# An attention block followed by an MLP on one core: modulation rows in a list of their own, other start conditions for weight preparation, and later reload times

## The chip, the cores and the metric

The kernel runs on one core of a Trainium2 chip. The core has a matrix engine (PE, with its weight loads shown as PEld), a vector engine (DVE), a scalar engine (ACT), a general engine (POOL) and an engine that issues the transfers (SP). The metric is the device time of one execution in microseconds. Three timed runs of the kernel before are given, and one further execution was profiled.

## The reference

One sequence of 2048 tokens of width 512. Six rows of modulation come from `c`; then attention with 32 heads of 16, and a mixer with a shift along the sequence and an MLP of width 1792.

```python
mod = (silu(c) @ w_mod).reshape(1, 6, 1, 512)
sa, ca, ga, sb, cb, gb = mod[:, 0], ..., mod[:, 5]
h = layernorm(x) * (1 + ca) + sa
x = x + ga * attention(h, wqkv, wo)          # 32 heads, softmax over 2048 keys
h = layernorm(x) * (1 + cb) + sb
y = h + shifted(gelu(layernorm(h) @ w1)) @ w2    # four groups of channels, shifts +1, -1, +2, -2
y = y + gelu(layernorm(y) @ w3) @ w4
return x + gb * y
```

## The kernel before

Everything is float32 in, float32 out. To multiply float32 matrices, each operand is split into a high part and a low rest, and three products are summed (`mm3`, L322 to L327). So each weight must be prepared once: loaded, split by ACT (high part) and DVE or POOL (rest). The attention weights stay in SBUF for their stage (`wp`, two buffers). The MLP weights and wo are cut into 20 `pieces` of two halves each, split, stored to a scratch tensor `Ws`, and read back later through a ring (`wr`).

**Stages.** A prologue normalizes x and prepares K of the first four heads. Then 64 attention units follow, in the order of four chunks of 512 queries by 16 pairs of heads. A unit has 16 steps: for each, two score matmuls (L956), two exponentials on ACT (L952), two products for the row maxima of a later unit (L940) with DVE reductions (L936), a halving of the low parts on POOL (L1004, or on ACT, L121) and the products with v (L1029, L1026). Beside the first 16 units ("the first quarter") lie the rest of the Q, K and V projections, the modulation rows and the weight pieces. Beside the other 48 units lies the MLP of the chunk just finished (`tail`), and after unit 63 the last chunk's MLP stands alone.

**Order.** No engine order comes from the compiler. The program itself holds a planner, `Sched` (L78 on): for each engine it keeps a planned time `T`, and instructions are emitted in the planned order. The attention steps are fixed; everything else is written as generators (lists of work that yield their PE cost or a condition) and as chains of operations for ACT, DVE and POOL. `fill` gives the generators a PE allowance after each block; `one` runs the first generator in the list whose condition holds, so earlier generators go first. `after(t, fn)` runs `fn` once the planned PE time reaches t. `dma` gives an estimated landing time: its size at 360 bytes per ns, behind SP's earlier transfers, plus 2200 ns (`DBW, DLAT`). All transfers are issued by SP, in the order in which they are emitted; a transfer whose buffer is still being read holds up what is behind it.

`drain(flag)` lets the planner step on, without attention work, until a flag is set. At the end of the first quarter it does that for v 1, kq 3, q 0, q 1 and `pieces` (L1529 on).

**Names.**
- `todo`: the projections in order: v 0, kq 1, kq 2, v 1, kq 3, q 0, q 1 (L790). `weights_gen` prepares their weights, `qkv_gen` computes them. There are two lists of the latter: (0, 3) and (1, 2, 4, 5, 6). v 0 and v 1 are the two halves of v; kq g is K of eight heads and Q of the first chunk for them.
- `staged` (L406): takes one of five buffers `wst`, issues a load into it and returns the planned landing time. All weight preparation and the modulation rows use it.
- `mod_gen` (L596): modulation rows, four pieces of 128 columns each, four matmuls per piece, result by DVE to `garow`, `sbrow`, `cbrow` or `gbrow`. `garow` and `sbrow` are the same tile: the first is used up by wo's pieces before the second is written.
- `pieces_load` (L802): loads the halves in the order w1, w3, wo, w2, w4. Before wo it makes `garow`, before w4 the other three rows. `pieces_gen` (L819): takes one of three buffers `wq`, then the scale by `vcol` (wo only, ACT, L831), by the row (wo and w4, POOL, L833), the high part (ACT, L843), the rest (POOL, L844), two stores.
- `load_v` (L912): reloads one quarter of v (`vst`) for the next unit, called through `sch.after` in `pv_part` (L1037).

Of the kernel before, what the change touches and what calls it, by code (L numbers as in the profile page):

```python
# [55 lines left out]
LATE = 1e9  # L56
# [7 lines left out]
NPT = 8  # L64
PLOAD = 3500.0
WLAT = 4000.0
WSR = 1
DBW, DLAT = 360.0, 2200.0
NST = 5
NWQ = 3  # L70
# [211 lines left out]
def cA(n=CH):  # L282
    return n / 1.2 + 52
# [11 lines left out]
def kernel(ctx, tc, A_x, A_wqkv, A_wo, B_w1, B_w2, B_w3, B_w4, c, w_mod, out):  # L295
# [58 lines left out]
    vcol = con.tile([P, 4], F32, name="vcol")  # L354
# [3 lines left out]
    cbrow = con.tile([P, D], F32, name="cbrow")  # L358
    sbrow = con.tile([P, D], F32, name="sbrow")
    gbrow = con.tile([P, D], F32, name="gbrow")  # L360
# [19 lines left out]
    sch = Sched()  # L380
    done = set()
# [18 lines left out]
    garow = sbrow  # L400
# [5 lines left out]
    def staged(src3):  # L406

        yield lambda: wst
        t = wst.pop(0)
        f = t.bitcast(F32)  # L410
        o = 0
        n = sum(x.shape[2] for x in src3)
        f3 = f.rearrange("p (k n) -> p k n", n=n)
        for x in src3:
            e = sch.dma(dma.dma_start, f3[:, :, o:o + x.shape[2]], x)
            o += x.shape[2]
        return t, f3, e

    def split_chain(t, hi, lo, *ops):
        f = t.bitcast(F32)  # L420
# [362 lines left out]

    def weights_gen():
        for i, (_, wt, a) in enumerate(todo):
            yield lambda: i <= ready["done"] + (("kq", 0) in done)
            ready[i] = yield from wt(a)


# [3 lines left out]
    def qkv_gen(*ids):  # L793
        for i in ids:
            gen, _, a = todo[i]
            yield lambda: i in ready
            yield from gen(ready.pop(i), a)
            ready["done"] += 1

    loaded = []  # L800

    def pieces_load():  # L802
        yield lambda: ("v", 0, 2) in done
        for i, (nm, src, nk, n) in enumerate(pieces):
            if i == order["wo"][0]:
                yield lambda: ("vcol", 0) in done and ("vcol", 1) in done
                yield from mod_gen((2, garow, 0.0))
            if i == order["w4"][0]:
                yield lambda: len(wqs) == NWQ and not loaded
                yield from mod_gen((3, sbrow, 0.0), (4, cbrow, 1.0), (5, gbrow, 0.0))  # L810
            src3 = kpn(src)
            for c in range(2):
                yield sch.wait(PLOAD)
                yield lambda: len(wst) > WSR or len(ready) + ready["done"] > len(todo)
                t, _, e = yield from staged([src3[:, c:c + 1] if nk == 2 else src3[:, 2 * c:2 * c + 2]])
                loaded.append((i, nm, c, t, e + WLAT))
        loaded.append(None)

    def pieces_gen():  # L819
        while True:  # L820
            yield lambda: loaded and wqs
            x = loaded.pop(0)
            if x is None:
                break
            i, nm, c, t, e = x
            w = wqs.pop(0)
            f = t.bitcast(F32)
            ops = []
            if nm == "wo":
                k = 2 * (i - order["wo"][0]) + c  # L830
                ops.append(("A", cA(), lambda f=f, k=k: act.activation(f, f, AF.Copy, scale=vcol[:, k:k + 1])))  # L831
            if nm in rows:
                ops.append(("G", cG(), lambda f=f, r=rows[nm]: pool.tensor_tensor(f, f, r, op=OP.mult)))  # L833

            def gone(t=t, w=w):
                wst.append(t)
                wqs.append(w)

            def store(i=i, c=c, w=w, f=f, gone=gone):
                for h, t in enumerate((w.bitcast(F32), f)):  # L840
                    e = sch.dma(dma.dma_start, Ws[i][:, h, 512 * c:512 * c + 512], t)
                sch.after(e, gone)
            sch.chain(*ops, ("A", cA(), lambda f=f, w=w: act.activation(w, f, AF.Copy)),  # L843
                      ("G", cG(), lambda f=f, t=t, w=w: pool.tensor_tensor(t, f, w, op=OP.subtract)),  # L844
                      (None, 0, store), ready=e)
        yield lambda: len(wqs) == NWQ
        done.add("pieces")

    def drain(flag):
# [17 lines left out]
    for ci in range(NC):  # L867
# [2 lines left out]
        ("A", cA(), lambda i=i: act.activation(hi[:, 2 * i:2 * i + 2], w0f[:, 2 * i:2 * i + 2], AF.Copy)),  # L870
        ("D", cD(), lambda i=i: dve.tensor_tensor(lo[:, 2 * i:2 * i + 2], w0f[:, 2 * i:2 * i + 2], hi[:, 2 * i:2 * i + 2],
                                                  op=OP.subtract)))], mark("w0"), ready=arr["w0"])
    for g in (mod_cols(), bounds(), ln1_T(), qk_first(hi, lo), weights_gen(), qkv_gen(0, 3), qkv_gen(1, 2, 4, 5, 6)):
        sch.add(g)
    drain(("q", 0, 0))
    for ci in range(NC):
# [26 lines left out]
    def load_unit(u):  # L903
# [3 lines left out]
        for j in range(2):  # L907
            h = 2 * pr + j
            load_rows(q, j, Qs, h, cs, slice(0, CH))
            load_rows(kst[u % 3], j, Ks, h, slice(0, S), slice(0, S))  # L910

    def load_v(u, i):  # L912

        if u < NU:
            sch.dma(dma.dma_start, vst[i], Vs[units[u][1], :, 4 * i:4 * i + 4])

    sm = Slots(NSM)
# [93 lines left out]
    def pv_part(s, lo):  # L1011


        u, kt = divmod(s, NKT)
        if kt == 0 and not lo:
            pv[u] = ap_.tile([P, CH], F32, name="pv", tag="v", bufs=1)
        v, acc = vst[kt // 4], pv[u]

        def mms():
            for j in range(2):  # L1020
                for i in range(2):
                    r = 64 * j + 32 * i
                    if lo:
                        n = 9 + DH if i else 1 + DH
                        c = 128 + 32 * j + 9 + DH
                        te.matmul(acc[r:r + n, :], v[:, (kt + i) % 4, c - n:c].bitcast(F16), pt[s + i].bitcast(F16)[:, j, 0::2],  # L1026
                                  start=False, stop=kt == NKT - 2, skip_group_check=True)
                    else:
                        te.matmul(acc[r:r + 32, :], v[:, kt % 4, r:r + 32], pt[s].bitcast(F16)[:, j, 1::2],  # L1029
                                  start=kt == 0, stop=False, skip_group_check=True)  # L1030
        e = sch.put("P", CCOL, 0.0, mms)
        if lo:
            for i in range(2):
                pts.append(pt.pop(s + i))
                e_low.pop(s + i)
            if kt % 4 == 2:
                sch.after(e + 300, partial(load_v, u + 1, kt // 4))  # L1037
            if kt == NKT - 2:
                acs.append((u, e + COUT))

# [391 lines left out]

    sch.share(sm, MOST0)
    sch.add(pieces_load(), 0)
    sch.add(pieces_gen(), 0)

    def budget(s):
# [36 lines left out]
    for k, blk in enumerate(blocks + [[]] * (LAG + CPER)):  # L1474
        if LENDS in blk:
            sch.most = MOST
        for x in blk:
            if x % 2 == 0:
                before(x // 2)
                if x >= 0 and x % 32 == 0:  # L1480
                    drain(("shift", x // 32))
        if acs:
            ac_copy()
        row = [divmod(x, 2) for x in blk if x < 2 * NS]
        s0 = row[0][0] if row else 0
        col = []
        if k >= LAG and (k % CPER == 0 or not blk):

            x = (blocks[min(k - LAG, len(blocks) - 1)] or [-1])[-1]
            while pvs and 2 * (pvs[0][0] + pvs[0][1]) < x:  # L1490
                if col and blk and pvs[0][0] % NKT == 0 and not pvs[0][1]:
                    break
                col.append(pvs.pop(0))
        t, start = CIN, 0.0
        need = sum((s >= 0) + (s + LEAD < NS) for s, _ in row)
        sch.flush(need)
        banks = sorted(sm.t)
        n = 0
        for s, i in row:
            n += (s >= 0) + (s + LEAD < NS)  # L1500

            start = max(start, banks[n - 1 + 2 * (s < 0)] - t)
            t += CROW
        t += CMID
        for s, i in col:
            start = max(start, pv_ready(s, i) - t)
            t += CCOL
        sch.gap(start)
        sch.flush(need)
        sch.T["P"] = max(sch.T["P"], start) + CIN  # L1510
        low = sorted(e_exp)
        for s, i in row:
            for fn in row_pair(s, i):
                fn()
        for s in low:
            p_low(s)
        sch.T["P"] += CMID
        for s, i in col:
            pv_part(s, i)
        if col:  # L1520
            sch.T["P"] += COUT
        for e in "ADG":
            sch.misc(e, max(sch.T["P"], sch.T[e]) + TOLE[e])
        due += sum(budget(x // 2) / 2 for x in blk) if blk else 3 * TAILB[-1] / 2
        if k % CPER == CPER - 1 or s0 < 0:
            sch.fill(due)
            due = 0.0
        if blk and blk[-1] == 2 * (NS // NC) - 1:
            for key in (("v", 1), ("kq", 3), ("q", 0), ("q", 1), "pieces"):  # L1529
                drain(key)  # L1530
            qpx.close()
            tpx = ExitStack()
            tp[0] = tpx.enter_context(tc.tile_pool(name="tp", bufs=1, side="right"))
# [47 lines left out]
```

## Time and profile before

| what | value |
|---|---|
| median of three runs | 2119.67 us (2115.31 to 2126.15) |
| profiled execution | 2129.35 us, span of its instructions 2127.6 us |
| granted TensorE clock, mean | 0.958 |

```profile
PE 1963.1 (92%) x14464; PEld 1163.4 (55%) x14464; DVE 1648.0 (77%) x2936; ACT 1536.5 (72%) x3320; POOL 1716.3 (81%) x1657
```

The line is the share of the span in which each engine was busy, with its number of instructions. It is a mean over stages that differ: the prologue to about 100 us, the first quarter to about 610 us, three more quarters to about 1960 us, and the last MLP. In the lines of the profile, L12 is line 12 of the program; a matmul carries the line of the helper that issues it (L323, L325, L327 are the three products of `mm3`), so groups are told apart by the tiles they write and read. A line such as "ACT pt L952 <- PE mb L940" says that the first waited for the second.

### The profile page before, as it was taken

What the parts mean: (1) busy time and instruction counts of PE and PEld (TensorE: products, weight loads), DVE (VectorE), ACT (ScalarE), POOL (GpSimd) and SP (SyncE); (2) the same over time, 40 slices, a digit from 0 to 9 for tenths busy, and PEclk for the clock granted to TensorE, in tenths of its full rate; (3) what the DMA queues carried; (4) which work ended last, traced back from release to release, by engine and by line L of the source; (5) the groups of instructions that cost most, each with busy time, mean ns of one, the idle gap of its engine ahead of it and who ended that gap; (6) DMA issues with size and microseconds to landing.
All of it is one profiled execution on the core that took longest, in us unless ns stands there. A gap on an engine that the chain in (4) does not pass through costs nothing.

```text
span 2127.6 us, 41619 instructions
## 1 busy us (share of the span) xinstructions
PE 1963.1 (92%) x14464; PEld 1163.4 (55%) x14464; DVE 1648.0 (77%) x2936; ACT 1536.5 (72%) x3320; POOL 1716.3 (81%) x1657
## 2 busy tenths in 40 slices
PE   6979897999859999999999999999989999999899
PEld 4645564554325555555545455555545555555788
DVE  7768686888749887888999888888898878882654
ACT  6367677767846877877868887877768797887353
POOL 4368788878887998988978999989879898998442
PEclk9989998999869998999999999999999999999999
DMA  5786876655573354454633444544534444443432
GB/s 194 187 248 203 222 185 195 177 144 144 144 252 93 88 127 100 136 118 136 155 66 87 108 100 108 138 117 108 172 96 104 108 104 108 112 121 101 176 138 85
DMA packets 228514, 292.69 MB, mean 138 GB/s; under 512 B 121264, under 2 KB 172976, under 8 KB 212016
## 3 DMA queue, kind: packets, MB, share of 16 engines
q1 hardware_dynamic: 228304, 290.02, 50.3%
q8 instruction: 115, 1.88, 0.4%
q14 instruction: 95, 0.78, 0.1%
HBM read 226.49 MB, written 62.91 MB: 136 GB/s over the span
## 4 chain that ended last, share of the span: by engine, by line
PE 58%; ACT 13%; DVE 13%; DMA 5%; POOL 5%; issue 3%; SPq 2%; POOLq 0%; ACTq 0%; DVEq 0%
PE mb L940 12%; PE pv L1029 9%; PE sc L956 9%; DVE mx L936 8%; ACT pt L952 7%; PE w L323 6%; PE w L325 5%; PE w L327 5%; PE pv L1026 4%; POOL pt L1004 2%; SPq L100 2%; DMA kst<-Ks 1%; DMA wst<-in_A_wqkv_dram 1%; PE ot L1056 1%; ACT pt L121 1%
## 5 line engine op out<-in xcount | busy, mean ns | idle before, releaser
L1004 POOL TENSOR_SCALAR pt<-pt 128x1024 f16<-128x1024 uint16 x983 | 1307.4, 1362 | 167.7 <-ACT pt L952 162.9
L936 DVE TENSOR_REDUCE mx<-mb 128x1 f32<-128x512 f32 x2048 | 1280.2, 683 | 209.6 <-PE mb L940 160.7
L952 ACT ACTIVATE pt<-sc 128x512 int32<-128x512 f32 x2048 | 1080.4, 607 | 303.7 <-PE mb L940 243.9
L940 PE MATMUL mb<-kst,qtl 48*128 48x512 f32 x2048 | 766.5, 462 | 90.2 <-ACT pt L952 49.1
L956 PE MATMUL sc<-qtl,kst 64*128 64x512 f32 x2048 | 733.5, 452 | 21.5 <-DMA qtl<-nm 8.8
L940 PEld LDWEIGHTS mb<-kst,qtl 48*128 48x128 f32 x2048 | 354.9, 197 | 302.8 <-ACT pt L952 113.8
L956 PEld LDWEIGHTS sc<-qtl,kst 64*128 64x128 f32 x2048 | 344.1, 190 | 183.3 <-ACT pt L952 55.1
L1029 PE MATMUL pv<-pt,vst 128*32 128x512 f16 x4096 | 366.4, 405 | 0.4 <-DMA vst<-Vs 0.4
L1026 PE MATMUL pv<-pt,vst 128*17 128x512 f16 (+1 forms) x2048 | 215.2, 403 | 0.3 <-ACT pt L121 0.2
L1029 PEld LDWEIGHTS <-vst 128*32 128x32 bf16 x4096 | 92.0, 96 | 164.1 <-issue 107.6
L323 PE MATMUL w<-A,wr 128*128 128x256 f32 (+2 forms) x576 | 176.4, 306 | 1.6 <-ACT A L317 1.4
L325 PE MATMUL w<-A,wr 128*128 128x256 f32 (+2 forms) x576 | 174.2, 302 | 1.1 <-DVE A L313 0.8
L1315 POOL TENSOR_TENSOR g<-xs,g 128x256 fp32r<-128x256 f32 (+2 forms) x144 | 103.4, 721 | 86.0 <-ACT g L1314 85.6
L327 PE MATMUL w<-A,wr 128*128 128x256 f32 (+2 forms) x576 | 172.3, 299 | 0.0
L323 PEld LDWEIGHTS w<-A,wr 128*128 128x128 f32 x576 | 113.4, 197 | 23.9 <-issue 13.9
L325 PEld LDWEIGHTS w<-A,wr 128*128 128x128 f32 x576 | 113.4, 197 | 19.3 <-issue 16.8
L327 PEld LDWEIGHTS w<-A,wr 128*128 128x128 f32 x576 | 113.5, 197 | 12.1 <-issue 12.1
L323 PE MATMUL w<-wr,g 128*128 128x512 f32 x288 | 119.5, 415 | 0.0
L327 PE MATMUL w<-wr,g 128*128 128x512 f32 x288 | 117.8, 409 | 0.3 <-POOL g L1315 0.3
L325 PE MATMUL w<-wr,g 128*128 128x512 f32 x288 | 116.6, 405 | 0.0
L1324 DVE SCALAR_TENSOR_TENSOR sq<-sq,w 128x256 f32<-128x256 f32 (+1 forms) x108 | 43.5, 403 | 80.2 <-ACT xs L1320 73.1
L1330 POOL TENSOR_TENSOR xs<-xs,sq 128x256 f32<-128x256 f32 (+1 forms) x108 | 75.8, 703 | 14.6 <-ACT sq L1329 14.0
(145 smaller groups left out, 2192.2 us busy)
## 6 DMA issues: line engine op xcount, KB each, us to landing
wr<-Ws SPq DMA_DIRECT2D x80, 1024.0 KB, 5.9
vst<-Vs SPq DMA_DIRECT2D x256, 192.0 KB, 2.7
kst<-Ks SPq DMA_DIRECT2D x126, 384.0 KB, 6.7
qtl<-Qs SPq DMA_DIRECT2D x128, 96.0 KB, 5.0
Vs<-vt SPq DMA_DIRECT2D x32, 384.0 KB, 4.8
Ws<-wq SPq DMA_DIRECT2D x40, 256.0 KB, 4.3
Ws<-wst SPq DMA_DIRECT2D x40, 256.0 KB, 4.2
wst<-in_B_w_dram SPq DMA_DIRECT2D x36, 256.0 KB, 4.2
```

Source lines behind the costliest of these rows:

```text
L323: te.matmul(o, lh, rh, start=first, stop=False)
L325: te.matmul(o, lh, rl, start=False, stop=False)
L327: te.matmul(o, ll, rh, start=False, stop=last)
L936: end = sch.crit("D", 605, e + PX, lambda: dve.reduce_max(mxs[u][:, j, g, c:c + 1], b, axis=AX.X))
L940: return ready, lambda: te.matmul(b, lhs, kst[u % 3][r, c * CH:(c + 1) * CH], start=True, stop=True), after
L952: ea = sch.crit("A", 480, e + PX, lambda: act.activation(pt[s][:, j], b, AF.Exp))
L956: return ready, lambda: te.matmul(b, kst[u % 3][r, kt * P:(kt + 1) * P], qst[u][r], start=True, stop=True), after
L1004: e_low[s] = XP["G"] + sch.crit("G", 1345, ready, lambda: pool.tensor_scalar(o, i, 0.5, 1.0, op0=OP.mult, op1=OP.mult))
L1026: te.matmul(acc[r:r + n, :], v[:, (kt + i) % 4, c - n:c].bitcast(F16), pt[s + i].bitcast(F16)[:, j, 0::2], start=False, stop=kt == NKT - 2 ...
L1029: te.matmul(acc[r:r + 32, :], v[:, kt % 4, r:r + 32], pt[s].bitcast(F16)[:, j, 1::2], start=kt == 0, stop=False, skip_group_check=True)
L1315: ("G", cG(n), lambda: pool.tensor_tensor(lo, xs, hi, op=OP.subtract)), (None, 0, end))
L1330: ("G", cG(n), lambda: pool.tensor_tensor(xs, xs, sq, op=OP.mult)), *tail_ops, bank=b)
```

## The change

Five parts, in the words of the diff:

1. The modulation rows get a generator of their own, `mod_rows`, which starts when kq 1 is done and goes ahead of the pieces in the list. It makes ga, gb and cb, then waits until wo's halves are stored, and makes sb. `pieces_load` waits for ga before wo and for gb before w4, and its start moves from three quarters of v 0 to kq 2.
2. The order of the projections: one list (1, 2, 3, 4, 5, 6) after v 0, so v 1 comes after kq 2 instead of in a list beside it; a weight is prepared when the projection two places ahead of it is done.
3. `staged` returns a landing time that is 4000 ns later (`WLAT`). For the pieces that is as before, where the same amount was added by `pieces_load`; for the projections and the modulation rows it is new.
4. v's reload is put 5000 ns (`VLATE`) behind the planned end of its readers, instead of 300 ns; should its first reader come sooner, it is issued there.
5. In the wait for a bank before the first score, a bank that has no planned end is left out of account.

```diff
+VLATE = 5000.0
...
-        return t, f3, e
+        return t, f3, e + WLAT
...
-            yield lambda: i <= ready["done"] + (("kq", 0) in done)
+            yield lambda: i < 1 or (("kq", 0) in done if i == 1 else ("todo", i - 2) in done)
             ready[i] = yield from wt(a)
...
             ready["done"] += 1
+            done.add(("todo", i))
...
+    def mod_rows():
+        yield lambda: ("kq", 1) in done
+        yield from mod_gen((2, garow, 0.0))
+        done.add("garow")
+        yield from mod_gen((5, gbrow, 0.0))
+        done.add("gbrow")
+        yield from mod_gen((4, cbrow, 1.0))
+        yield lambda: all(("wo", 2 * i + c) in done for i in order["wo"] for c in range(2))
+        yield from mod_gen((3, sbrow, 0.0))
+        done.add("mods")
+
     def pieces_load():
-        yield lambda: ("v", 0, 2) in done
+        yield lambda: ("kq", 2) in done
         for i, (nm, src, nk, n) in enumerate(pieces):
             if i == order["wo"][0]:
-                yield lambda: ("vcol", 0) in done and ("vcol", 1) in done
-                yield from mod_gen((2, garow, 0.0))
+                yield lambda: ("vcol", 0) in done and ("vcol", 1) in done and "garow" in done
             if i == order["w4"][0]:
-                yield lambda: len(wqs) == NWQ and not loaded
-                yield from mod_gen((3, sbrow, 0.0), (4, cbrow, 1.0), (5, gbrow, 0.0))
+                yield lambda: "gbrow" in done
...
-                loaded.append((i, nm, c, t, e + WLAT))
+                loaded.append((i, nm, c, t, e))
...
                 sch.after(e, gone)
+                done.add((nm, 2 * i + c))
...
-        yield lambda: len(wqs) == NWQ
+        yield lambda: len(wqs) == NWQ and "mods" in done
         done.add("pieces")
...
-    for g in (mod_cols(), bounds(), ln1_T(), qk_first(hi, lo), weights_gen(), qkv_gen(0, 3), qkv_gen(1, 2, 4, 5, 6)):
+    for g in (mod_cols(), bounds(), ln1_T(), qk_first(hi, lo), weights_gen(), qkv_gen(0), qkv_gen(1, 2, 3, 4, 5, 6)):
...
+    vnext = set()
+
     def load_v(u, i):
-        if u < NU:
+        if (u, i) in vnext or not u:
+            vnext.discard((u, i))
             sch.dma(dma.dma_start, vst[i], Vs[units[u][1], :, 4 * i:4 * i + 4])
...
+        load_v(u, kt // 4) if (u, kt // 4) in vnext else None
         v, acc = vst[kt // 4], pv[u]
...
-                sch.after(e + 300, partial(load_v, u + 1, kt // 4))
+                if u + 1 < NU:
+                    vnext.add((u + 1, kt // 4))
+                sch.after(e + VLATE, partial(load_v, u + 1, kt // 4))
...
     sch.add(pieces_load(), 0)
+    sch.add(mod_rows(), 0)
     sch.add(pieces_gen(), 0)
...
-            start = max(start, banks[n - 1 + 2 * (s < 0)] - t)
+            free = banks[n - 1 + 2 * (s < 0)]
+            start = max(start, (free if free < LATE else banks[n - 1]) - t)
```

More of the change, by code (lines that the diff above doesn't have):

```diff
@@ L837, in gone, with store @@
                 wqs.append(w)
-            def store(i=i, c=c, w=w, f=f, gone=gone):
+            def store(i=i, c=c, w=w, f=f, gone=gone, nm=nm):
                 for h, t in enumerate((w.bitcast(F32), f)):
```

## The prediction, made before the changed kernel was timed

> **What bounds the kernel now.** I first read the share of busy time by engine and the waits, then stretches of the span one by one, because the first quarter (attention units 0 to 15, beside which the weights are prepared) differs from the other three.
>
> ```profile
> 187.80:349.10 161.30, 141.19 (x1112) 84.89 (x1110) 115.45 (x203) 120.64 (x259) 134.55 (x120) 0.96 0.78 213
> 382.70:561.90 179.20, 169.71 (x1340) 90.41 (x1338) 149.91 (x264) 129.86 (x260) 151.06 (x127) 0.98 0.56 144
> 205.00:584.00 379.00, 346.26 (x2664) 191.83 (x2668) 295.98 (x515) 279.48 (x571) 317.00 (x272) 0.96 0.66 174
> 584.00:609.40 25.40, 0.79 (x9) 0.00 (x0) 0.17 (x1) 6.16 (x11) 20.96 (x18) 0.50 0.76 272
> 609.40:640.00 30.60, 28.69 (x202) 15.25 (x202) 24.27 (x42) 21.91 (x44) 25.25 (x22) 0.86 0.83 240
> 640.00:1090.00 450.00, 430.78 (x3333) 242.95 (x3326) 379.00 (x672) 351.89 (x784) 395.90 (x390) 0.96 0.46 116
> 1560.00:1960.00 400.00, 384.38 (x2983) 216.34 (x2984) 306.23 (x547) 320.58 (x704) 360.08 (x350) 0.98 0.42 105
> ```
>
> Columns: stretch, its length, busy time of PE, PEld, DVE, ACT, POOL, granted TensorE clock, DMA share, GB/s. In the later quarters PE is busy for 384.4 of 400 us: there the kernel is bound by PE, with POOL (90%) and ACT (80%) close behind. In the first quarter it is not: from 205 to 584 us PE is busy only 91%, and from 584 to 609 us it stands still. PE's timeline, with the gap before an instruction in brackets, names the holes:
>
> ```profile
> 137.08 1.28 PE L940 MATMUL mb<-kst,qtl 48*128 48x512 f32 x2 [8.27 <-ACT pt L952]
> ...
> 259.48 0.79 PE L604 MATMUL mr<-wst,sil 128*128 128x128 f32 x3 [4.07 <-DMA wst<-in_w_mod_dram]
> ...
> 349.75 1.12 PE L1056 MATMUL ot<-ident,ac 128*128 128x128 f32 x4 [11.16 <-ACT ac L1045]
> ...
> 609.44 0.79 PE L940 MATMUL mb<-kst,qtl 48*128 48x512 f32 x1 [24.65 <-ACT pt L952]
> ```
> These four gaps make 48.2 us. "ACT pt" is only the last link. Behind the first and the 11.2 us one ACT itself sat on a weight that had not landed:
>
> ```profile
> 135.91 0.63 ACT L425 ACTIVATE wp<-wst 128x512 fp32r<-128x512 f32 x1 [6.16 <-DMA wst<-in_A_wqkv_dram]
> ...
> 341.82 0.63 ACT L843 ACTIVATE wq<-wst 128x512 fp32r<-128x512 f32 x1 [1.76 <-DMA Ws<-wq]
> 346.58 0.63 ACT L425 ACTIVATE wp<-wst 128x512 fp32r<-128x512 f32 x1 [4.12 <-DMA wst<-in_A_wqkv_dram]
> 348.58 0.63 ACT L425 ACTIVATE wp<-wst 128x512 fp32r<-128x512 f32 x1 [1.38 <-DMA wst<-in_A_wqkv_dram]
> ```
>
> Behind the 24.65 us gap the chain that ended last shows something else: the quarter's end drains `pieces`, and the MLP weight halves are scaled (L833) and split (L844) on POOL one after the other, with attention halted.
>
> ```profile
> 583.59 1.94 POOL wst L833 x2
> 585.52 0.45 issue
> 585.97 1.28 POOL wst L844
> ...
> 588.47 1.41 POOL wst L844 x2
> ...
> 607.02 1.23 POOL wst L833
> 608.27 0.63 ACT wq L843
> 608.90 0.49 ACT pt L952
> ```
>
> Why they are late is seen when the work on `wq` (one ACT operation for each of the 40 halves) and on `mr` (matmuls of the modulation rows, eight for each of 16 row pieces) is counted by stretch:
>
> ```profile
> 100.00:205.00 105.00, 6.84 (x11) 13.40 (x11) 0.93 0.77 222
> 205.00:390.00 185.00, 9.70 (x15) 21.27 (x16) 0.94 0.77 210
> 390.00:530.00 140.00, 0.00 (x0) 0.00 (x0) 1.00 0.55 140
> 530.00:584.00 54.00, 3.26 (x5) 6.38 (x5) 0.90 0.55 137
> 584.00:612.00 28.00, 5.66 (x9) 11.37 (x9) 0.50 0.75 266
> ```
> ```profile
> 390.00:530.00 140.00, 13.54 (x96) 11.85 (x96) 3.38 (x12) 1.00 0.55 140
> ```
>
> For 140 us no half is touched (x0), since the list of pieces stands in its own generator behind 12 modulation row pieces (96 matmuls). Of the last 14 halves five are split by 584 us, and nine fall into the drain.
>
> **The change, part by part.** *Rows by their own list, and pieces later.* `pieces_load` starts when kq 2 is done instead of after three quarters of v 0, so about 198 us instead of 115:
>
> ```profile
> 115.52 0.42 SPq L100 DMA_DIRECT2D wst<-in_B_w_dram  x1
> ...
> 194.88 0.90 SPq L100 DMA_DIRECT2D Qs<-qk  x2
> ```
> ```profile
> 123.24 0.62 ACT L843 ACTIVATE wq<-wst 128x512 fp32r<-128x512 f32 x1
> ```
>
> The first load of a half is the 115 us one; the stores at 194.9 us are kq 2's last, and land some 3 us later. The 140 us pause goes. None of the new conditions is a wait on an engine; they only hold back the planner's lists, so nothing queues behind them. So 40 halves have 198 to 584 us = 386 us, 9.6 us each. Before, 26 halves went through by 390 us; the 11 of the first row took about 82 us from the first at 123 us, 7.5 us each; 40 x 7.5 = 300 us, and at 8.6 (15% worse, since the weights of v 1, kq 3 and q share the five `wst` buffers) 344 us, ending at 542 us. I expect the drain to be empty. With the halves move their 120 transfers on SP's queue (a load and two stores each), past the loads of K, Q and v; DMA share is 0.55 to 0.77 there, so I give that no price of its own. The twelve row pieces (13.5 us PE, 3.4 us DVE in the 140 us) move from 390 to 530 to about 130 to 350 us with the same instructions: 0.
>
> The work itself stays and now lies beside attention. From 205 to 609.4 us, 404.4 us, PE is busy 346.3 + 0.8 = 347.1 us, POOL 317.0 + 21.0 and ACT 279.5 + 6.2, together 623.7. To it come the 11 halves that were done before 205 us: 13.4 POOL + 6.8 ACT, making 643.9. Two floors follow. By PE: 347.1 at the share of the last stretch (384.38 / 400 = 0.961) is 361 us. By POOL and ACT together, between which the planner moves the low halves of pt: 643.9 at (360.08 + 320.58) / 400 = 1.70 is 378 us; at the 1.66 of 640 to 1090 us it is 388 us. The higher floor decides; I take 378, so **-26 us**, ends 361 (-43) and 395 (-9; the rate of the worst of these rows with one hole left). This contains the drain and the holes at 259 and 349 us.
>
> *v half 1 after kq 2, not beside it.* It is due in unit 7, about 355 us, and its 16 tiles start after kq 2, at 198 us, against 191 before. The instructions are the same, so 0; what hides the delay is that slack of over 150 us. If it were used up, attention would stand in a drain for v as it does for the pieces (nearest row: 24.65 us).
>
> *Arrival 4 us later for all weights.* Of ACT's 6.16 us wait at 136 us at most 4 go, so the PE gap of 8.27 shrinks by 4: **-4 us** (ends 0 and -8). The modulation rows get it too (the PE gap of 4.07 us at 259 us), but that lies in the term above. In the prologue the same 4 us delays kq 1 and v 0, while q and k of group 0 occupy PE: **+1 us** (0 to 4).
>
> A rule speaks against this term. First the trace, issues with their size and the median time to landing:
>
> ```profile
> wst<-in_B_w_dram SPq DMA_DIRECT2D x36, 256.0 KB, 4.2
> ...
> wst<-in_w_mod_dram SPq DMA_DIRECT2D x16, 256.0 KB, 5.2
> ...
> wst<-in_A_wqkv_dram SPq DMA_DIRECT2D x8, 256.0 KB, 7.2
> ```
>
> The planner counts 0.7 + 2.2 us for them. The Trainium skill, page "DMA: Bandwidth & Descriptors", section "Anatomy of one DMA — SWDGE (gpsimd) path", fits a copy at 2.0 us plus its bytes at 436 GB/s, an estimate of 2.6 us for 256 KB; by it the old figure is ample, the term would be 0 and the sum 2089 us. The medians above, 4.2 to 7.2 us, disagree.
>
> *Clock behind the holes.* From 609.4 to 640 us the granted clock is 0.86; 14% of 30.6 us is 4.3 us; I take **-3 us** (0 to -5). The Trainium skill, "TensorE: Matmul & The Clock Gate", Part 1, says that an idle window of some 3.4 us halves the clock until a busy window of that length has passed; by it each of the four holes costs some 1.7 us after its end, an estimate of 7 us in all, and a sum of 2081 us. The 0.50 in the row of 584 us agrees with the halving.
>
> *v's reload 5 us later.* What SP waits for, and what PE waits for through SP:
>
> ```profile
> SPq L100 <- PE pv L1026: 704.7, 167, 11.1
> SPq L100 <- PE w L327: 186.1, 45, 22.7
> ```
> ```profile
> PE sc L956 <- DMA qtl<-nm: 8.8, 7, 1.8
> ```
> ```profile
> vst<-Vs SPq DMA_DIRECT2D x256, 192.0 KB, 2.7
> ```
>
> SP's queue stands for 705 us behind v's readers, but what PE loses to queued transfers is small: 8.8 us at the shift rows. Behind a v load stand shift rows, K and Q of the next unit and `wr`. Half of 8.8, less what the first term holds: **-3 us** (0 to -6). SP will in part only wait for the next item (the L327 row). The fallback for a bank that is taken concerns rows before the first score alone: 0.
>
> **Sum:** -26 - 4 + 1 - 3 - 3 = -35 us. The profiled execution took 2129.35 us (span 2127.6, 1.8 around it), 9.7 above the median of the three timed runs, 2119.67; the terms are differences, so I subtract them from the median: **2085 us**.
>
> **Rivals.** (1) *POOL and ACT take it back.* The halves come back as delays of exponentials and low halves. For it: POOL is the second engine everywhere, and 187.8 to 349.1 us, where pieces, v and kq 3 ran together, shows 84% on POOL with PE at 88%. Against: (134.55 + 120.64) / 161.3 = 1.58 leaves room up to 1.70. At 395 us for the stretch and nothing else but -4 and -3: 2119.7 - 16 = 2104 us.
> (2) *The issue is late, not the arrival, or pieces still spill over.* SP issued the weight of 135.9 us only at 130.5, behind other transfers:
>
> ```profile
> 130.54 2.31 SPq L100 DMA_DIRECT2D wst<-in_A_wqkv_dram  x2
> ```
>
> If the later plan only shifts with it, the 17 us of holes stay, and a few halves are left at the end, each worth 25.4 / 9 = 2.8 us. With three left: 2085 + 17 + 8 = 2110 us, which is within 0.5% of before (0.5%, 10.6 us, is about what a measurement of this kernel can tell from no change).
> (3) *Slower: v arrives late.* The second stretch of the first fence runs from the end of unit 7 to that of unit 14, so a unit takes 179.2 / 7 = 25.6 us, and a v quarter is free for 12 of its 16 steps, 19.2 us. Less 5 and its landing (2.7) there are 11.5 us for SP's backlog. Where SP is behind by more than that (the 22.7 us above happens, though mostly it waits under 11.1), PE waits at the first pv matmul. If a tenth of the 252 reloads came 2 us late that is 50 us: 2135 us. Against it: PE waits for vst only 0.4 us before, by the group's row, and a queue that blocks less runs ahead.
>
> ```profile
> L1029 PE MATMUL pv<-pt,vst 128*32 128x512 f16 x4096 | 366.4, 405 | 0.4 <-DMA vst<-Vs 0.4
> ```
>
> (4) *PE floor reached*, holes all gone: 2119.7 - 43 - 8 - 5 - 3 = 2061 us.
>
> **Chances.** Forecast (2070 to 2098 us) 0.57; rival 1: 0.18; rival 2: 0.12; rival 3: 0.06; rival 4: 0.07. Faster by over 0.5% (under 2109 us): forecast, rivals 1 and 4 = 0.82, less 0.02 for rival 1's upper edge; within 0.5%: rival 2 and that edge less what falls beyond, 0.13; slower: 0.07. The range leaves out rival 3, the upper half of rival 2 and half of rival 4: 2062 to 2111 us.
>
> **What would show it.** Right: no PE gap over 5 us near 570 to 610 us; x0 for `wq` in the last 10 us before the boundary; `mr` matmuls between 130 and 350 us; ACT's waits for wst<-in_A_wqkv_dram (11.7 us in the three rows above) under 4; SP's wait for pv L1026 down by more than half, PE's for qtl<-nm under 5 us; the stretch from kq 2's end to unit 16 near 378 us with POOL at 90%. Wrong: a drain that still holds PE, units of over 29 us on average between 200 and 580 us without PE gaps over 2 us (rival 1), or PE waiting for vst<-Vs (rival 3).

## The result and the profile after

The changed kernel takes 2072.11 us (median of four runs, 2067.63 to 2073.44) against 2120.64 us before; the ratio is 0.9767, 95% interval 0.9738 to 0.9797. The forecast was 2085 us, range 2062 to 2111. The profiled execution has a span of 2071.7 us (before 2127.6) and a mean granted clock of 0.974 (before 0.958). Each later run was timed beside the kernel before, whose median was then between 2119 and 2125 us, so a difference between the medians of two runs is uncertain by some us; where the ratios to before give a clearly different figure, it is added.

First the windows of the changed kernel over the first quarter and over units 16 to 63; columns as in the prediction: stretch, length, busy time of PE, PEld, DVE, ACT, POOL, clock, DMA share, GB/s.

```profile
190.00:555.00 365.00, 346.91 (x2674) 191.60 (x2672) 297.02 (x515) 297.67 (x612) 343.34 (x294) 0.99 0.80 224
560.40:1899.90 1339.50, 1285.71 (x9955) 722.53 (x9954) 1105.39 (x1959) 1056.47 (x2323) 1190.48 (x1156) 0.98 0.46 114
```

PE is now busy 95% of the first quarter (346.91 of 365), close to the 96% behind it. There is no stretch like 584 to 609 us before. The windows of the work on `wq` show why: ACT's and POOL's operations on the halves no longer stand at x0 from 390 to 530 us, and none is left for a drain.

```profile
100.00:205.00 105.00, 0.00 (x0) 0.00 (x0) 0.97 0.65 170
205.00:390.00 185.00, 14.16 (x23) 28.34 (x22) 0.97 0.85 238
390.00:530.00 140.00, 11.67 (x18) 22.48 (x17) 1.00 0.78 229
```

The forty high parts are made between 229 and 529 us, and the quarter ends without a drain. Of the three waits that the prediction followed, ACT's on the weights has gone from the group (0.0 us idle), PE's for the shift rows is down from 8.8 us to 0.6, and SP's for v's readers from 704.7 to 434.5. From the groups by line, and from the waits of PE and of SP:

```profile
L426 ACT ACTIVATE wp<-wst 128x512 fp32r<-128x512 f32 x14 | 9.0, 641 | 0.0
```
```profile
PE sc L971 <- DMA qtl<-nm: 0.6, 1, 0.6
PE pv L1045 <- DMA vst<-Vs: 6.2, 2, 4.3
```
```profile
SPq L101 <- PE pv L1042: 434.5, 99, 10.3
SPq L101 <- PE w L328: 243.9, 57, 23.7
```

New is that PE waits for v itself, 6.2 us in two places. One is at the start of unit 16, where three ring loads and four loads of x now go out ahead of v; PE's timeline, with the gap in brackets:

```profile
576.11 1.04 PE L1045 MATMUL pv<-pt,vst 128*32 128x512 f16 x8 [4.31 <-DMA vst<-Vs]
```

Where the time went is read from the copy that ends each unit (ACT, `ac<-pv`): the starts of the copy of unit 0, unit 15 and unit 63 split each profiled span into four parts. All kernels of this study are in the table; times in us. A name with undo is the changed kernel with one part taken back, one with only is the kernel before with one part alone, and the others are named at their experiments. A row is one profiled execution, so differences of 2 or 3 us between rows mean little.

| kernel | end of unit 0 | units 1 to 15 | units 16 to 63 | last MLP | span |
|---|---|---|---|---|---|
| before | 149.5 | 464.3 | 1344.7 | 169.1 | 2127.6 |
| changed | 137.6 | 422.8 | 1339.5 | 171.8 | 2071.7 |
| undo_rows | 136.0 | 462.4 | 1330.8 | 171.5 | 2100.6 |
| undo_arrival | 146.6 | 432.0 | 1336.0 | 171.4 | 2086.0 |
| undo_v_late | 141.0 | 431.3 | 1339.3 | 168.6 | 2080.1 |
| undo_v_order | 135.4 | 426.9 | 1338.9 | 168.2 | 2069.5 |
| only_rows | 150.9 | 441.0 | 1332.1 | 170.4 | 2094.3 |
| only_arrival | 137.9 | 480.3 | 1336.5 | 168.2 | 2122.9 |
| only_v_late | 147.6 | 446.1 | 1337.2 | 171.1 | 2101.9 |
| pieces_early | 139.1 | 424.2 | 1342.3 | 171.7 | 2077.3 |
| less_pool | 137.6 | 409.6 | 1341.4 | 170.1 | 2058.7 |
| v_quarter | 141.0 | 427.6 | 1336.8 | 171.7 | 2077.1 |
| arrival_6 | 144.4 | 423.0 | 1317.6 | 172.1 | 2057.1 |
| ring_6 | 135.6 | 423.0 | 1322.9 | 171.6 | 2053.0 |

Of the 55.9 us between the two spans, 11.9 lie before the end of unit 0, 41.5 in units 1 to 15 and 5.2 behind them; the last MLP gives 2.7 back. Up to the end of unit 0 the two traces hold equally many matmuls, 622, so the 11.9 us there are time and not work that was put off: PE stands idle for 24.2 us in place of 34.4.

### The profile page after: what moved, and what is told of

Read it like the earlier page. It is cut to its first block, busy times and chain, and to the rows that moved or that the text cites. A ratio compares the mean times of both kernels' runs of the same rounds, so it can differ in the third digit from the quotient of the medians.

```text
span 2071.7 us, 41454 instructions
## 1 busy us (share of the span) xinstructions
PE 1955.8 (94%) x14464; PEld 1157.0 (56%) x14464; DVE 1646.8 (79%) x2936; ACT 1537.8 (74%) x3332; POOL 1708.3 (82%) x1651
## 4 chain that ended last, share of the span: by engine, by line
PE 60%; DVE 16%; ACT 12%; POOL 5%; DMA 3%; issue 3%; SPq 1%; POOLq 0%; ACTq 0%; DVEq 0%
PE mb L955 13%; DVE mx L951 10%; PE pv L1045 9%; PE sc L971 9%; ACT pt L967 6%; PE w L324 6%; PE w L326 6%; PE w L328 6%; PE pv L1042 4%; POOL pt L1019 3%; ACT pt L122 1%; PE ot L1074 1%; DVE tst L335 1%; DVE sq L1342 1%; SPq L101 1%
## 5 line engine op out<-in xcount | busy, mean ns | idle before, releaser
L971 PEld LDWEIGHTS sc<-qtl,kst 64*128 64x128 f32 x2048 | 341.4, 188 | 171.5 <-ACT pt L967 51.8
L328 PE MATMUL w<-A,wr 128*128 128x256 f32 (+2 forms) x576 | 172.5, 300 | 0.0
L328 PEld LDWEIGHTS w<-A,wr 128*128 128x128 f32 x576 | 113.7, 197 | 12.4 <-issue 12.4
L328 PE MATMUL w<-wr,g 128*128 128x512 f32 x288 | 117.8, 409 | 0.4 <-POOL g L1333 0.3
```

The lines of the kernel that those rows point to most:

```text
L328: te.matmul(o, ll, rh, start=False, stop=last)
L971: return ready, lambda: te.matmul(b, kst[u % 3][r, kt * P:(kt + 1) * P], qst[u][r], start=True, stop=True), after
```

## The experiments

Theory: the drain at the end of the first quarter comes from the pause in the list of halves, so the rows' own list is the main part; the arrival removes holes in which an engine stands on a weight and the work queued behind it stands too; v's reload gives a few us. Rivals: the arrival or SP's freed queue does it; or POOL and ACT take the moved work back. First each part was undone in the changed kernel, then done alone in the kernel before. Part 5, the bank, was not taken alone; it goes with the arrival.

### The rows back in the pieces' list

```diff
             if i == order["wo"][0]:
-                yield lambda: ... and "garow" in done
+                yield lambda: ...
+                yield from mod_gen((2, garow, 0.0))
             if i == order["w4"][0]:
-                yield lambda: "gbrow" in done
+                yield lambda: len(wqs) == NWQ and not loaded
+                yield from mod_gen((3, sbrow, 0.0), (4, cbrow, 1.0), (5, gbrow, 0.0))
```

> The changed kernel with one part undone: the modulation rows stand in the pieces' list again (pieces still start at kq 2). Theory (the 140 us pause and the drain it causes are the main gain): halves start at 198 us and then pause for twelve row pieces, so more than nine halves fall into the drain; the PE gap at the end of the first quarter is 25 us or more, total 2095 to 2125 us. Rival (arrival and reload times are the main gain): total within 10 us of the changed kernel's 2072 us.

Measured: 2105.03 us, 0.9927 of before (0.9896 to 0.9958): 33 us more than the changed kernel. PE's timeline and the windows of `wq`:

```profile
594.01 0.79 PE L946 MATMUL mb<-kst,qtl 48*128 48x512 f32 x1 [42.85 <-ACT pt L958]
```
```profile
551.00:594.00 43.00, 8.79 (x14) 16.86 (x14) 0.55 0.69 226
```

All 14 halves of w4 stand in the drain, 42.85 us. The theory holds. 42.85 / 14 = 3.1 us a half, and before it was 24.65 / 9 = 2.7.

### The short arrival again

```diff
-        return t, f3, e + WLAT
+        return t, f3, e
...
-                loaded.append((i, nm, c, t, e))
+                loaded.append((i, nm, c, t, e + WLAT))
```

> The changed kernel with the longer arrival undone for projections and modulation rows (kept for the pieces). Theory: the drain stays away, the holes in which ACT or PE stands on a weight not landed come back in part, 8 to 20 us: 2080 to 2092 us, with waits for wst in the trace. Rival (SP's freed queue makes the weights land early enough): no such waits, 2070 to 2076 us.

Measured: 2088.78 us, 0.9868 (0.9827 to 0.9909), 16.7 us more than the changed kernel (21 by the ratios), and as the theory says. ACT's wait for these weights is there again, and a modulation row stops PE at 131 us, since its matmuls stand in PE's queue ahead of attention:

```profile
L426 ACT ACTIVATE wp<-wst 128x512 fp32r<-128x512 f32 x14 | 8.6, 630 | 8.1 <-DMA wst<-in_A_wqkv_dram 8.1
```
```profile
130.88 1.40 PE L605 MATMUL mr<-wst,sil 128*128 128x128 f32 x5 [7.17 <-DMA wst<-in_w_mod_dram]
```

Not every gap of this run is a weight's: the largest inside the stretch, 5.96 us at 326 us, lies behind ACT's wait of 3.97 us for a store of v (Vs<-vt).

By the Trainium skill's fit in "DMA: Bandwidth & Descriptors", section "Anatomy of one DMA — SWDGE (gpsimd) path", quoted in the prediction, the old arrival figure would have been ample and this run equal to the changed kernel; the measurement decides against that. The Trainium skill gives that fit for transfers issued through gpsimd. Those here are issued by SP, and 256 KB of weights took 4.2 to 7.2 us in the kernel before, so it is carrying the fit over that fails.

### v's reload early, and v 1 beside kq 2, again

```diff
-VLATE = 5000.0
+VLATE = 300.0
```

> The changed kernel with v's reload 300 ns behind its readers again. Theory: little rests on it, 2072 to 2078 us; SP's wait for pv rises from 435 us to about 700; the two PE waits for vst (1.9 and 4.3 us) shrink. Rival (a free SP queue is what removes the holes at 137 and 350 us): PE gaps over 5 us come back in the first quarter, 2085 us or more.

Measured: 2080.55 us, 0.9803 (0.9767 to 0.984), 8.4 us more than the changed kernel, more than the theory's 6 at most; the intervals overlap, so that is not clear of noise. SP's wait for v's readers is 682.9 us and PE's for the shift rows 8.4 us, much as before, and PE's for v falls from 6.2 us to 1.8. No gap over 3.6 us came back in the first quarter, so SP's queue is not what made the large holes.

```diff
-            yield lambda: i < 1 or (("kq", 0) in done if i == 1 else ("todo", i - 2) in done)
+            yield lambda: i <= ready["done"] + (("kq", 0) in done)
...
-    ... qkv_gen(0), qkv_gen(1, 2, 3, 4, 5, 6)
+    ... qkv_gen(0, 3), qkv_gen(1, 2, 4, 5, 6)
```

> The changed kernel with the projections in two lists again, v 1 beside kq 2, and the old condition for preparing a weight. Theory: the same work on the same engines, no due time near: 2068 to 2078 us. Rival (v beside k overloads ACT and DVE): 2080 us or more, with units of over 33 us between 190 and 350 us.

Measured: 2071.85 us, 0.9772 (0.9742 to 0.9802), no difference that can be measured: the order of the projections and the later half of v show no effect.

### One part alone on the kernel before

The same edits on the kernel before: the list of rows with pieces from 115 us; the longer arrival (with the fallback for a bank); the later reload.

> The kernel before with one part alone: the modulation rows in their own list (pieces still start at 115 us, short arrival, early reload). Theory: the drain goes, the holes on weights not landed stay: 2088 to 2098 us. Rival (the halves' POOL work comes back as longer units): 2105 us or more without a drain.

Measured: 2095.13 us, 0.9889 (0.9873 to 0.9904). The drain is gone, as the theory says. The holes changed, which it does not say: those of 8.27 and 11.16 us near 137 and 350 us are no longer there, the largest gap around 350 us is 3.92 us, and ACT's wait for the weights of the projections falls from 17.5 to 7.8 us. One hole is new: the rows now load early, with the short arrival, and PE stands on the first of them for 11 us. So unit 0 ends no earlier than before (150.9 against 149.5 us), and the hole near 350 us goes by the list as well as by the arrival.

```profile
134.89 1.41 PE L604 MATMUL mr<-wst,sil 128*128 128x128 f32 x5 [11.10 <-DMA wst<-in_w_mod_dram]
...
354.61 0.89 PE L950 MATMUL mb<-kst,qtl 48*128 48x512 f32 x2 [3.92 <-DMA kst<-Ks]
```

> The kernel before with the longer arrival alone (and the fallback for a bank that is taken, which it needs). Theory: the 25 us gap of the drain stays, the gaps of 8.3, 4.1 and 11.2 us shrink: 2100 to 2112 us. Rival (lists and arrival only work together): 2115 us or more.

Measured: 2127.41 us, 1.0047 (1.0025 to 1.0068): slower than before. Here the theory's total falls and the rival's holds. Unit 0 ends at 137.9 us, 11.6 earlier than before, so the hole at 137 us is closed. But units 1 to 15 take 16 us longer. PE's timeline and the windows of all engines over the drain:

```profile
613.88 0.79 PE L940 MATMUL mb<-kst,qtl 48*128 48x512 f32 x1 [43.87 <-ACT pt L952]
```
```profile
570.00:613.90 43.90, 0.03 (x6) 0.02 (x2) 0.00 (x0) 9.36 (x16) 33.55 (x28) 0.50 0.68 228
```

28 operations on POOL, two for each of 14 halves. In the one list each row piece now waits for a landing time that is 4 us later, and the halves stand behind the rows. The windows of `mr` show the rows later: before, all 96 of their matmuls lay between 390 and 530 us (the prediction's row).

```profile
390.00:530.00 140.00, 10.85 (x79) 9.63 (x80) 2.55 (x9) 1.00 0.57 143
530.00:570.00 40.00, 2.64 (x19) 2.07 (x18) 0.85 (x3) 0.94 0.39 80
```

All of w4 falls into the drain, which grows from 24.65 to 43.87 us. The part that gains 16.7 us with the rows' own list loses without it.

> The kernel before with v's later reload alone. Theory: 3 to 10 us less, 2110 to 2118 us, with PE's waits for the shift rows (qtl<-nm) gone and the drain unchanged. Rival (SP's queue caused the holes): gaps of 8.3 and 11.2 us gone, 2105 us or less.

Measured: 2102.01 us, 0.9921 (0.9894 to 0.9947), 17 us less than before instead of 3 to 10. The waits for the shift rows are gone, and the two big holes remain (8.48 and 12.22 us), so the rival falls. Of the rest 10 us are the drain, which is shorter and holds five halves (the window reaches past its end at 589 us, but the five high parts lie inside it):

```profile
589.35 0.79 PE L944 MATMUL mb<-kst,qtl 48*128 48x512 f32 x1 [14.56 <-ACT pt L956]
```
```profile
575.00:612.00 37.00, 3.15 (x5) 6.28 (x5) 0.77 0.88 283
```

Four more halves got through before it because the rows ahead of them were done earlier: their last matmuls start at 489.3 us instead of 525.4, and w4's first high part at 518.7 instead of 551.2. Why the rows came forward is not shown; the reload times also shift the planner's own picture of SP's queue, and with it the order of everything else. A theory that a part acts only where its wait stands cannot foresee this.

### Is the later start of the pieces worth something?

```diff
     def pieces_load():
-        yield lambda: ("kq", 2) in done
+        yield lambda: ("v", 0, 2) in done
```

> The changed kernel with the start of the pieces at three quarters of v 0 again, 115 us. Theory: the later start is not what gains, as the halves only have to be done by the end of the quarter: 2068 to 2080 us. Rival (the later start relieves ACT and POOL while K, Q and v are prepared): 2084 us or more.

Measured: 2074.55 us, 0.9789 (0.9763 to 0.9815). The interval overlaps that of the changed kernel, so the later start shows no worth of its own, as the theory has it.

### What the moved work costs beside attention

```diff
-            if nm in rows:
+            if False:
                 ops.append(("G", cG(), lambda f=f, r=rows[nm]: pool.tensor_tensor(f, f, r, op=OP.mult)))
...
-                      ("G", cG(), lambda f=f, t=t, w=w: pool.tensor_tensor(t, f, w, op=OP.subtract)),
```

> The changed kernel without the pieces' two POOL operations (the scale by a row and the low rest are left out, some 75 us of POOL in the first quarter). If POOL and ACT together set the pace there, as the forecast's second floor has it, 75 us at 1.7 per us are some 40 us: 2030 to 2045 us. If PE sets it, the work lies in gaps and little is gained: 2060 to 2070 us.

Measured: 2058.25 us, 0.9682 (0.9646 to 0.9718), 13.9 us less than the changed kernel (18 by the ratios), between the two expectations and nearer to PE's; unit 15 ends 13.2 us earlier. Its windows:

```profile
190.00:542.00 352.00, 339.15 (x2673) 189.19 (x2672) 298.33 (x515) 279.75 (x580) 294.82 (x252) 1.00 0.83 233
```

Against the changed kernel's 365 us POOL has lost 48.5 busy us and ACT 17.9, PE is busy 96% instead of 95%, and the stretch is 13 us shorter: PE's idle time falls by 5 us, and its busy time by 8. So some 75 us of POOL work cost 13 us of time; most of it lay in gaps.

### Two attempts to go further

```diff
-                sch.after(e + VLATE, partial(load_v, u + 1, kt // 4))
+                sch.after(e + (300 if u % NP == NP - 1 else VLATE), partial(load_v, u + 1, kt // 4))
```

> The changed kernel with v's reload 300 ns behind its readers for the first unit of a query chunk alone (there the ring and x are loaded ahead of v, and PE waited 4.3 us for vst at 576 us). Theory: that gap goes, 2066 to 2071 us. Rival (SP's queue then holds up the shift rows instead): 2072 us or more.

Measured: 2069.78 us (2062.68 to 2078.94), 0.9747 (0.9718 to 0.9775): no difference to the changed kernel that can be measured. The 4.31 us gap is gone, a wait of 1.47 us for the shift rows stands near its place, and unit 15 ends 8 us later in the profiled run, which was the longest of the six.

```diff
-WLAT = 4000.0
+WLAT = 6000.0
```

> The changed kernel with 6 us in place of 4 for the arrival (also of the pieces and the ring). If what is left of waits on weights (the 4.0 us of ACT on a half at 320 us) costs time: 2064 to 2070 us. If the halves get so late that a drain comes back, as in the run with the arrival alone: 2076 us or more, with a PE gap at the end of the first quarter.

Measured: 2061.76 us, 0.9709 (0.9676 to 0.9742), faster than expected, and not where it was expected: unit 15 ends 6.9 us later than in the changed kernel and units 16 to 63 take 21.9 us less. `WLAT` is also the ring's figure, the time after which a block of MLP weights may be used. The last run gives the longer time to the ring alone.

```diff
+RLAT = 6000.0
...
-                    self.q.append((halves(w, pieces[i][2]), pl, e + WLAT))
+                    self.q.append((halves(w, pieces[i][2]), pl, e + RLAT))
```

> The changed kernel with 6 us of arrival for the ring of MLP weights alone, 4 us for everything prepared in the first quarter. In the run with 6 us for all, unit 15 ended 7 us later than in the changed kernel and the 48 units behind it took 22 us less. Theory (the gain is the ring's, the loss the first quarter's): unit 15 ends at 560 us as in the changed kernel, units 16 to 63 take 1315 to 1322 us instead of 1339, total 2047 to 2055 us. Rival (the 22 us come from how the first quarter ended, not from the ring): units 16 to 63 take 1335 us or more, total 2068 us or more.

Measured: 2054.57 us, 0.9678 (0.965 to 0.9707), the fastest kernel here that leaves nothing out, 17.5 us below the changed one, and the intervals do not overlap. Unit 15 ends at 558.5 us and units 16 to 63 take 1322.9 us, as the theory has it (0.9 us past its upper end); the copies of units 15 and 63 in ACT's timeline, and the windows between them:

```profile
558.53 0.66 ACT L1064 ACTIVATE ac<-pv 128x512 f32<-128x512 f32 x1
...
1881.41 0.58 ACT L1064 ACTIVATE ac<-pv 128x512 f32<-128x512 f32 x1
```
```profile
558.50:1881.40 1322.90, 1277.30 (x9942) 718.78 (x9941) 1104.57 (x1958) 1056.03 (x2322) 1187.32 (x1152) 0.98 0.46 116
```

PE's idle time fell from 53.8 us (1339.50 - 1285.71) to 45.6 and its busy time by 8.4, with the same matmuls and the same granted clock of 0.98. In neither trace does an engine wait for a load of `wr`, so it is not a late landing that was mended. How the later use of ring blocks changes the order so that it fits better stays open.

## Why the prediction was right, point by point

**The pause and the drain.** Right. Putting the rows back brings a drain of 42.85 us; the list alone, with nothing else, removes it. A half left at the end costs 2.7 to 3.1 us in four kernels (9, 14, 14 and 5 halves), against the 2.8 in rival 2. The mechanism is a list that waits behind other work which the planner itself put ahead of it, not an engine at its limit. The signs came: 96 row matmuls between 130 and 350 us, nothing of `wq` in the last 20 us of the quarter, and no gap of PE at its end. The pace was off: the high parts began at 229 us and came 7.7 us apart, where 198 and 8.6 had been forecast, and ended at 529 instead of 542.

**The stretch of the first quarter, -26 us.** Too small. Attention stood at 205 us where the changed kernel stands at about 189 (unit 2 was 69% done: 167.2 + 0.69 x 31.6, from the starts of the copies of units 1 and 2), and the stretch that took 404.4 us ends with unit 15, 53.3 us earlier than before. So it took 404.4 - 53.3 + 16 = 367 us, not 378, although it had more to do: by 189 us PE has issued 963 matmuls (161.0 us busy), where it had issued 992 (167.6 us) by 205 us before, so 6.6 us of the 16 are work put off into the stretch. The step that failed is the second floor, "by POOL and ACT together": the rate of 1.70 read from 1560 to 1960 us was taken as what the two can do. In the changed kernel they do (297.67 + 343.34) / 365 = 1.76, and with 75 us less POOL work the time falls by 13, not by 40. 1.70 was what those quarters asked for, not what the engines could give. The time lies near PE's floor: 361 was the first floor, or (347.1 + 6.6) / 0.961 = 368 with the work put off, an estimate from these windows, and 367 came. POOL was busy 94% of the stretch, not the 90% forecast, and yet, by the run with less POOL work, did not set its length.

**Arrival, -4 us before 205 us and +1 in the prologue.** Mechanism right, size wrong. The argument was that of a 6.16 us wait "at most 4 go". With the arrival alone unit 0 ends 11.6 us earlier, in the changed kernel 11.9, and neither has the 8.27 us gap. What the sum missed is that moving the weight's split back in ACT's queue does more than shorten its wait by 4 us: attention's exponentials go ahead of it. In the changed kernel ACT's part of this split comes at 139.61 us, behind them and without a wait; before it stood ahead of them, at 135.91 us, with 6.16 us of wait. SP also issues the load earlier, at 126.0 us instead of 130.5, and so it does with the arrival alone; why is not shown. The prologue's cost of 1 us does not show. The hole near 350 us, which the prediction counts in the stretch, went with the rows' list alone too.

**Clock, -3 us.** The mean clock rose from 0.958 to 0.974, and in the three drains looked at (0.50 before, 0.55 and 0.50 in the runs above) it was low, so the term has the right sign. It can't be told apart from the gaps that it follows.

**v's reload, -3 us.** Right in kind, small in size: 8.4 us when undone (intervals that overlap), 17 us when done alone, of which 10 are a smaller drain. The predicted sign in the trace, SP's wait for pv down by more than half, did not come (down 38%); SP waits for the ring's and the scores' readers instead, 243.9 us for w L328 after 186.1 before. Rival 3, v arriving late, exists in the small: 6.2 us. The landing of 2.7 us in its working was that of the kernel before; in the changed kernel the median for the same loads is 4.8 us.

**v's order, 0.** Right: 0.9772 against 0.9767.

**Rivals.** Rival 1 (work comes back) is 13 us of what could have been 40; the 84% that it gives for POOL is 83% (134.55 / 161.3). Rival 2 fell: the holes closed and no half spilled over. Its 17 us of holes is not worked out there; the three holes on weights make 23.5. Rival 4, the PE floor at 2061 us, was passed by a kernel that leaves nothing out only with the longer ring time, and that gains in the other quarters.

**Total.** -35 forecast, -48.5 between the medians (-55.9 between the profiled spans): the stretch of the first quarter gave 37 instead of 26, and the time ahead of it 16 instead of 3, clock and reload included in both. So the direction and the mechanism of the main term were foreseen, and both sizes were too small, by 11 and 13 us. That the result still lies inside the forecast's own band (2070 to 2098), 2 us from its edge, owes something to the width of the band. The parts don't add: alone they make -1.11%, +0.47% and -0.79%, together -2.33%.

## What to carry to other kernels

A halt at the end of a stage is read backwards: find the work that runs inside it, then the stretch in which that work stood at x0, then what stood ahead of it in its own list; each unit left over here cost about 3 us, so the halt can be priced from a count. When a wait is fixed by placing an instruction later, look at what else stands in that list: a longer arrival gained 17 us with the rows in their own list, and lost time without it. A busy share read from another stage shows what that stage asked of an engine, and is no floor for this one.

## What was not expected of the hardware

One matmul group that waited for a transfer stopped all of PE, attention behind it included: 4.07 us before, 7.17 and 11.10 us in two of the runs. And a queue that waits much need not cost much: SP stood for 682.9 us behind v's readers with the early reload and for 434.5 without it, in kernels that differ in nothing else, and the time differed by 8 us, with intervals that overlap.
